# Pinned ScalarE and VectorE queues, a different x load, and a reordered start and end in a DFT + gated MLP kernel

## The chip, the cores and the metric

The kernel runs on one core of one Trainium2 chip. The metric is the device time of one launch in microseconds (us). Five engines have their own instruction queues: PE (TensorE, matmuls; "PEld" is its weight load), DVE (VectorE), ACT (ScalarE), POOL (GpSimd) and SP (SyncE). Transfers go through DMA queues that an engine issues to.

## The reference

```python
x : (8, 3008, 256) f32     w_in : (256, 2048)     w_out : (2048, 256)
X   = fft(fft(x, axis=1), axis=2).real      # along the sequence, then along the channels
h   = X.reshape(24064, 256) @ w_in
g   = h * cos(h)
out = g @ w_out                             # (24064, 256) f32
```

## The kernel before

The DFT along the sequence is done with matmuls on folded inputs (sums and differences of x rows that are gathered in normal and reversed order). The DFT along the channels is folded into `w_in`, giving `Wc` and `Ws`. The MLP then runs in 376 steps: 47 tiles of 256 columns with 8 steps each. A batch is 47 steps, and beside these steps the next batch is loaded, folded (16 folds on DVE, 0.95 us each) and transformed (four groups of matmuls).

One step does this, with the names that the profile shows:

- PE: even matmuls (`hp<-Rr,Wc`, and `hp<-Rl,Wl`, which adds one extra channel in bf16 limbs), odd matmuls (`hp<-Ir,Ws`, into the same PSUM tile), and the second layer's matmuls of four steps earlier (`Ma` to `Md`), of which two groups read a tile `d`.
- ACT: `pt` copy (-2·hp, between the even and the odd matmuls), `h` copy (after the odd ones), rounding, sine, `d` copy.
- DVE: "minus" (`h<-pt,hp`), subtraction of the rounded value (`r<-h,r`), product (`h<-h,r`), two sums.
- POOL: it issues an adding DMA `d<-h`, once a step.

The odd matmuls must wait for the `pt` copy, because they write on into the tile that it reads. Three parts matter below. First the load of x:

```python
    def load_x(b):
        L = [spool.tile([128, 6 * ND], FP, tag=f"xl{j}", bufs=1, ...) for j in range(4)]
        for j in (2, 1):                       # rows in reversed order: a table of row numbers
            nc.gpsimd.indirect_dma_start(
                out=L[j], out_offset=None, in_=xflat,
                in_offset=bass.IndirectOffsetOnAxis(ap=ix[:, j - 1 : j], axis=0),
                element_offset=b * SEQ * ND,
            )
        # row 0 of L[1] is not what the table gives: it is written over
        nc.gpsimd.dma_start(out=L[1][0:1, 0 : 5 * ND], in_=xrows(b, SEQ - 5, 1, 1, 5))
        nc.gpsimd.dma_start(out=L[1][0:1, 5 * ND :], in_=xrows(b, 0, 1, 1, 1))
        nc.sync.dma_start(out=L[0], in_=xrows(b, 0, 6, 128))
        nc.sync.dma_start(out=L[3], in_=xrows(b, HALF, 6, 128))
```

Second, the step's work on ACT and DVE. Only the matmuls are pinned to source order; the instructions of ACT and DVE are not, and are scheduled by the compiler:

```python
        # in mlp1_even, after the even matmuls
        nc.scalar.activation(out=pt, in_=hp, func=AF.Copy, bias=0.0, scale=-2.0)
    ...
        # in mlp1_odd, after the odd matmuls
        nc.scalar.copy(out=h[:, 0:512], in_=hp)
        nc.vector.tensor_tensor(out=h[:, 1023:511:-1], in0=pt, in1=hp, op=ALU.add)   # minus
        act_chain(h, 1024)              # ACT round, DVE subtract, ACT sine, DVE product
        nc.vector.tensor_tensor(out=A[5], in0=A[3], in1=A[2], op=ALU.add)            # sums
        nc.vector.tensor_tensor(out=A[4], in0=A[0], in1=A[5], op=ALU.add)
        d = spool.tile([128, 512], FP, tag="d", bufs=DB, name="d")                   # DB = 4
        nc.scalar.copy(out=d, in_=h[:, 0:512])
        nc.gpsimd.dma_start(out=d, in_=h[:, 768:1280], accum_op=ALU.add)
```

Third, the loop and what runs beside it:

```python
    at(2, load_ext)                     # the extra channel, as 4-byte elements
    at(8, fold_ext); at_dft(10, dft_ext)
    for n in range(3): at(12 + n, lambda n=n: limb_ext(n))
    at(14, lambda: spread_ext(0, RUN))  # gives Rl, first needed at step 16
    for b in range(1, NB):
        s0 = (b - 1) * steps_b
        at(s0 + (7 if b == 1 else 1), lambda b=b: start_batch(b))            # load_x
        for i, key in enumerate(FOLDS):
            at(s0 + 10 + i * 3 // 4, lambda key=key: state["ops"][key]())
    ...
    for i in range(total + LAG):        # LAG = 4
        for fn in side.get(i, ()):
            fn()
        ... mlp1_even(step i)
        ... mlp2(step i - LAG, between=odd)   # odd matmuls before its fourth matmul group
```

## Time and profile before

| | before |
|---|---|
| time | 2174.08 us, median of 2 runs (2171.41 to 2176.75) |
| span of the profiled run, mean granted TensorE clock | 2171.1 us, 0.988 |
| PE busy | 95% |
| first even matmul / step 16 (by its Rl matmul) / last matmul | 60.2 / 166.6 / 2162.2 us |
| 47 steps in the middle | about 257 us |
| step when PE alone limits it | 4.97 us |

The page's first lines give the span, then for each engine its busy time, the share of the span and the number of instructions:

```profile
span 2171.1 us, 26759 instructions
PE 2071.5 (95%) x9540; PEld 1688.2 (78%) x9540; DVE 1723.5 (79%) x2419; ACT 1461.0 (67%) x1976; POOL 353.5 (16%) x414
```

The view of waits lists which engine and tile waited, for whom, and then microseconds in total, how often, and the longest. These are PE's rows:

```profile
PE Mb L378 <- issue: 21.7, 1, 21.7
PE hp L653 <- ACT pt L642: 19.6, 63, 0.9
...
PE hp L632 <- DMA Rl<-r_124: 8.5, 1, 8.5
PE db L831 <- DVE h L690: 7.4, 1, 7.4
```

PE is close to full. Its waits are at the start (the first transform, 21.7; the extra channel's `Rl` at step 16, 8.5), at the end (7.4, the middle tokens), and a small one for the `pt` copy.

In some stretches a step is longer than 4.97 us. The timeline of ACT shows start, duration, engine, line, operation and what it waited for in brackets; this is one such stretch:

```profile
2049.90 0.58 ACT L642 ACTIVATE pt<-hp 128x512 f32<-128x512 f32 x1
2051.29 1.15 ACT L687 ACTIVATE r<-r,halfpi 128x1024 f32<-128x1024 f32 x1 [0.81 <-DVE r L684]
2052.34 0.57 ACT L666 COPY h<-hp 128x512 f32<-128x512 f32 x1
2053.73 0.62 ACT L672 COPY d<-h 128x512 f32<-128x512 f32 x1 [0.82 <-DVE h L690]
2054.32 1.06 ACT L681 ACTIVATE r<-h 128x1024 int32<-128x1024 f32 x1
2055.29 0.58 ACT L642 ACTIVATE pt<-hp 128x512 f32<-128x512 f32 x1
```

From one `pt` copy to the next is 5.39 us. The order is pt, sine, h copy, d copy, round. The commonest step of the kernel is PE's own 4.97 us (144 of 375, from one `hp<-Rl` matmul to the next step's); 5.39 us is found 45 times.

### The profile page before, as it was taken

How to read it: one execution, taken by the hardware profiler on the slowest of the kernel's cores; microseconds unless marked ns; L12 is line 12 of the kernel's file. 1: busy time of each engine (PE TensorE's matmuls, PEld its weight loads, DVE VectorE, ACT ScalarE, POOL GpSimd, SP SyncE). 2: the span in 40 equal slices, each digit the busy share in tenths (PEclk: the TensorE clock that was granted, in tenths of full speed). 3: DMA queues.
4: the chain of work that ended last, by engine and by line, in shares of the span. 5: the costliest groups of instructions: out<-in, count | busy, mean ns of one | idle time of the engine just before them, and what ended most of it. 6: DMA issues, size and time to landing. Idle time of an engine off the chain costs nothing.

```text
span 2171.1 us, 26759 instructions
## 1 busy us (share of the span) xinstructions
PE 2071.5 (95%) x9540; PEld 1688.2 (78%) x9540; DVE 1723.5 (79%) x2419; ACT 1461.0 (67%) x1976; POOL 353.5 (16%) x414
## 2 busy tenths in 40 slices
PE   4878999999999999999999999999999999999988
PEld 1667888877888788887888878887788887888866
DVE  3788778887779778898788977799777987788756
ACT  1656667776676667776677766777667776777755
POOL 1111111111111111111111111111111111111111
PEclk8999999999999999999999999999999999999999
DMA  9934333343333433333333434334333332233323
GB/s 227 68 69 88 55 83 68 64 92 64 76 66 59 89 79 66 65 62 84 84 68 64 89 57 93 61 61 93 71 76 59 63 69 54 55 63 69 62 44 64
DMA packets 212822, 159.85 MB, mean 74 GB/s; under 512 B 159171, under 2 KB 159196, under 8 KB 212175
## 3 DMA queue, kind: packets, MB, share of 16 engines
q0 software_dynamic: 56960, 111.22, 27.8%
q1 hardware_dynamic: 153494, 46.83, 10.6%
q8 instruction: 75, 1.23, 0.2%
q10 hardware_dynamic: 2232, 0.07, 0.1%
q14 instruction: 61, 0.49, 0.1%
HBM read 34.71 MB, written 24.78 MB: 27 GB/s over the span
## 4 chain that ended last, share of the span: by engine, by line
PE 44%; DVE 29%; ACT 19%; issue 5%; DMA 2%; DVEq 0%; SPq 0%; ACTq 0%
DVE h L690 10%; DVE r L684 8%; ACT r L687 8%; PE hp L653 8%; ACT r L681 7%; PE hp L620 7%; PE Md L720 7%; PE Mc L720 6%; PE Mb L720 6%; PE Ma L720 3%; PE db L378 3%; PE da L378 3%; ACT d L672 3%; DVE h L667 2%; PE hp L632 2%
## 5 line engine op out<-in xcount | busy, mean ns | idle before, releaser
L690 DVE SCALAR_TENSOR_TENSOR h<-h,r 128x1024 f32<-128x1024 f32 x377 | 454.9, 1217 | 204.7 <-ACT r L687 202.9
L673 POOL DMA_DIRECT2D d<-h x376 | 321.9, 886 | 1711.3 <-ACT r L681 641.1
L687 ACT ACTIVATE r<-r,halfpi 128x1024 f32<-128x1024 f32 x377 | 431.2, 1146 | 180.4 <-DVE r L684 178.0
L684 DVE TENSOR_TENSOR r<-h,r 128x1024 f32<-128x1024 f32 x377 | 454.7, 1218 | 116.9 <-ACT r L681 116.3
L681 ACT ACTIVATE r<-h 128x1024 int32<-128x1024 f32 x377 | 391.7, 1053 | 84.7 <-DVE h L667 83.7
L653 PE MATMUL hp<-Ir,Ws 127*128 127x256 f32 x1504 | 396.1, 389 | 22.4 <-ACT pt L642 19.6
L620 PE MATMUL hp<-Rr,Wc 128*128 128x256 f32 x1504 | 387.1, 380 | 1.7 <-DVE h L667 1.3
L672 ACT COPY d<-h 128x512 f32<-128x512 f32 x376 | 231.8, 617 | 180.9 <-DVE h L690 170.9
L653 PEld LDWEIGHTS hp<-Ir,Ws 127*128 127x128 f32 x1504 | 268.1, 189 | 105.3 <-ACT pt L642 75.6
L620 PEld LDWEIGHTS hp<-Rr,Wc 128*128 128x128 f32 x1504 | 284.7, 190 | 50.1 <-DVE h L667 5.4
L667 DVE TENSOR_TENSOR h<-pt,hp 128x512 f32<-128x512 f32 x376 | 252.4, 681 | 51.1 <-ACT h L666 50.6
L642 ACT ACTIVATE pt<-hp 128x512 f32<-128x512 f32 x376 | 221.1, 588 | 94.1 <-PE hp L632 91.6
L666 ACT COPY h<-hp 128x512 f32<-128x512 f32 x376 | 217.2, 578 | 95.6 <-PE hp L653 89.5
L720 PE MATMUL Mc<-h,T_118 128*128 128x256 f32 x752 | 224.6, 380 | 4.7 <-DVE X L751 4.7
L720 PE MATMUL Mc<-d,T_120 128*128 128x256 f32 x752 | 223.4, 379 | 4.6 <-DVE h L667 3.5
L720 PE MATMUL Mb<-h,w_88 128*128 128x256 f32 x752 | 224.4, 380 | 3.3 <-DVE X L751 3.3
L720 PE MATMUL Md<-h,T_121 128*128 128x256 f32 x752 | 224.6, 380 | 2.9 <-DVE X L751 1.9
L720 PE MATMUL Ma<-h,w_88 128*128 128x256 f32 x752 | 225.1, 381 | 0.0
L720 PE MATMUL Mb<-h,T_119 128*128 128x256 f32 x752 | 224.1, 380 | 0.0
L720 PE MATMUL Md<-d,w_88 128*128 128x256 f32 x752 | 224.1, 380 | 0.0
L720 PEld LDWEIGHTS Mc<-h,T_118 128*128 128x128 f32 x752 | 142.9, 191 | 25.7 <-issue 6.3
L720 PEld LDWEIGHTS Mc<-d,T_120 128*128 128x128 f32 x752 | 141.7, 189 | 25.7 <-DVE h L667 3.9
(347 smaller groups left out, 1917.6 us busy)
## 6 DMA issues: line engine op xcount, KB each, us to landing
d<-h POOLq DMA_DIRECT2D x376, 256.0 KB, 3.3
out_dram<-tr SPq DMA_DIRECT2D x252, 64.0 KB
h<-in_moe_w_in_dram SPq DMA_DIRECT2D x4, 512.0 KB
w_88<-in_moe_w_out_dram SPq DMA_DIRECT2D x8, 256.0 KB
out_dram<-tr SPq DMA_DIRECT2D x128, 4.0 KB
out_dram<-tr SPq DMA_DIRECT2D x32, 56.0 KB
out_dram<-tr SPq DMA_DIRECT2D x32, 48.0 KB
out_dram<-tr SPq DMA_DIRECT2D x32, 40.0 KB
```

The costliest lines, as they stand in the source:

```text
L620: nc.tensor.matmul(hp[:, i * TW : (i + 1) * TW], lhsT=Wc[:, f * 128 : (f + 1) * 128], rhs=Rr[:, pos : pos + TW], start=(i == 0), stop=Fals ...
L642: nc.scalar.activation(out=pt, in_=hp, func=AF.Copy, bias=0.0, scale=-2.0)
L653: nc.tensor.matmul(hp[:, i * TW : (i + 1) * TW], lhsT=Ws[0:127, f * 128 : (f + 1) * 128], rhs=Ir[:, pos : pos + TW], start=False, stop=Tru ...
L666: nc.scalar.copy(out=h[:, 0:512], in_=hp)
L667: nc.vector.tensor_tensor(out=h[:, 1023:511:-1], in0=pt, in1=hp, op=ALU.add)
L672: nc.scalar.copy(out=d, in_=h[:, 0:512])
L673: nc.gpsimd.dma_start(out=d, in_=h[:, 768:1280], accum_op=ALU.add)
L681: nc.scalar.activation(out=k, in_=h[:, 0:n], func=AF.Copy, bias=0.25, scale=1.0)
L684: nc.vector.tensor_tensor(out=r[:, 0:n], in0=h[:, 0:n], in1=k, op=ALU.subtract)
L687: nc.scalar.activation(out=r[:, 0:n], in_=r[:, 0:n], func=AF.Sin, bias=halfpi, scale=TWO_PI)
L690: nc.vector.scalar_tensor_tensor(out=h[:, 0:n], in0=h[:, 0:n], scalar=TWO_PI, in1=r[:, 0:n], op0=ALU.mult, op1=ALU.mult,)
L720: nc.tensor.matmul(T.M[bank][:, half * TW : (half + 1) * TW], lhsT=lhsT[:, s], rhs=rhs, start=(s == 0 and n in (0, 1, 3, 5)), stop=(s == 7 ...
```

## The change

The intent is to start the steps earlier, to end sooner, and to run the queues of ACT and DVE as a fixed software pipeline over three steps, so that no instruction stands in front of one that is needed sooner. The core of the diff:

```diff
-DB = 4
+DB = 3
 ...
-    neg = SEQ - 5 - 6 * p
-    neg[0] = SEQ - 6
+    neg = SEQ - 5 - 6 * (p + 1)
+    neg[127] = 0
 ... load_x: row 0 no longer gathered and written over; 127 rows are gathered
-        for j in (2, 1):
+        for j, p0 in ((2, 0), (1, 1)):
             nc.gpsimd.indirect_dma_start(
-                out=L[j],
+                out=L[j][p0:],
                 out_offset=None,
                 in_=xflat,
-                in_offset=bass.IndirectOffsetOnAxis(ap=ix[:, j - 1 : j], axis=0),
+                in_offset=bass.IndirectOffsetOnAxis(
+                    ap=ix[: 128 - p0, j - 1 : j], axis=0
+                ),
                 element_offset=b * SEQ * ND,
             )
-        nc.gpsimd.dma_start(out=L[1][0:1, 0 : 5 * ND], in_=xrows(b, SEQ - 5, 1, 1, 5))
-        nc.gpsimd.dma_start(out=L[1][0:1, 5 * ND :], in_=xrows(b, 0, 1, 1, 1))
+        nc.sync.dma_start(out=L[1][0:1, 0 : 5 * ND], in_=xrows(b, SEQ - 5, 1, 1, 5))
+        nc.sync.dma_start(out=L[1][0:1, 5 * ND :], in_=xrows(b, 0, 1, 1, 1))
 ... start: w_out loaded after all DFT constants; limb masks first on ACT's queue; the
     weight row goes to memory and back on POOL's queue, its limbs are made
     (row_to_limbs) behind the first folds and at step 1 rather than ahead of the folds
 ... mlp2: the odd matmuls two places later, Md<-h ahead of Mc<-d
-            if n == 3 and between is not None:
+            if n == 5 and between is not None:
 ... end: the middle tokens in five stages, one a step, rather than all at once
-    at(last, middle_tokens)
+    for i, fn in enumerate((middle_1, middle_2, middle_3, middle_4, middle_5)):
+        at(last + i + (i > 2), fn)
 ... folds: one a step (before: four in three steps)
-            at(s0 + 10 + i * 3 // 4, lambda key=key: state["ops"][key]())
+            at(s0 + 10 + i, lambda key=key: state["ops"][key]())
 ... the loop; every instruction below is now pinned to source order on its engine
     for i in range(total + LAG):
+        stage(i - 1, minus)                    # DVE
         for fn in side.get(i, ()):             # folds and evacuations among them
             fn()
+        stage(i - 2, act_sine)                 # ACT        (calls shortened here)
+        stage(i - 1, rounded)                  # ACT
+        stage(i - 2, act_product)              # DVE
+        stage(i - 2, sums)                     # DVE, then ACT's d copy and the DMA d<-h
+        stage(i - 1, act_rest)                 # DVE        subtraction
+        if ahead < i:
+            stage(i, mlp1_even)                # PE
+            stage(i, copy_even)                # ACT        pt copy
 ...     second layer of step i - LAG on PE, with mlp1_odd(i) inside it
+        stage(i, copy_plus)                    # ACT        h copy
```

More of the change, by code (lines that the diff above doesn't have):

```diff
@@ L130 @@
     nc.sync.dma_start(out=ix, in_=IX_dr.ap())
+    LC = cpool.tile([128, 4], FP, tag="LC")
+    nc.scalar.dma_start(out=LC, in_=LC_dr.ap())
     def load_x(b):
@@ L181 @@
             MC[ri, kodd] = m
-        if kodd == 0:
-            w2r = w2.rearrange("p (q e a j) -> p q e a j", e=2, a=4, j=32)
-            wor = moe_w_out.rearrange("(q p) (a e j) -> p q e a j", p=128, e=2, j=32)
-            for e in range(2):
-                for a in range(4):
-                    nc.sync.dma_start(out=w2r[:, :, e, a], in_=wor[:, :, e, a])
-    LC = cpool.tile([128, 4], FP, tag="LC")
-    nc.sync.dma_start(out=LC, in_=LC_dr.ap())
+    w2r = w2.rearrange("p (q e a j) -> p q e a j", e=2, a=4, j=32)
+    wor = moe_w_out.rearrange("(q p) (a e j) -> p q e a j", p=128, e=2, j=32)
+    for e in range(2):
+        for a in range(4):
+            nc.sync.dma_start(out=w2r[:, :, e, a], in_=wor[:, :, e, a])
     halfpi = cpool.tile([128, 1], FP, tag="halfpi")
@@ L205 @@
     Wl = cpool.tile([128, NDFF], BF, tag="Wl")
-    nc.gpsimd.memset(Rl, 0.0)
-    nc.gpsimd.memset(Wl, 0.0)
+    nc.vector.memset(Wl, 0.0)
+    nc.vector.memset(Rl, 0.0)
     T1 = cpool.tile([128, NF // 2, 128], FP, tag="T1")
@@ L252, in fold_weights, with load_row, row_to_limbs @@
             if q % 2:
-                c0 = (q - 1) * 512
-                half_limbs(slice(c0, c0 + 1024), c0 // 128)
+                load_row(q // 2)
         with nc.allow_non_contiguous_dma(reason="one row to columns"):
-            nc.scalar.dma_start(
+            nc.gpsimd.dma_start(
                 out=wex, in_=wx_dr.rearrange("o (f p) -> p (o f)", p=128)
             )
-    def half_limbs(cols, f0):
-        nc.scalar.dma_start(out=wx_dr[:, cols], in_=Ws[127:128, cols])
+    def load_row(half):
+        cols = slice(half * 1024, (half + 1) * 1024)
+        nc.gpsimd.dma_start(out=wx_dr[:, cols], in_=Ws[127:128, cols])
         wf = spool.tile([8, 128], FP, tag="wf", bufs=2, name="wf")
-        nc.scalar.dma_start(
+        nc.gpsimd.dma_start(
             out=wf, in_=wx_dr[0, cols].rearrange("(f p) -> f p", p=128)
         )
+        state["wf", half] = wf
+    def row_to_limbs(half):
+        cols = slice(half * 1024, (half + 1) * 1024)
         l3 = spool.tile([8, 3, 128], BF, tag="l3", bufs=2, name="l3")
-        split_limbs(wf, [l3[:, j] for j in range(3)])
-        for j in range(3):
-            nc.scalar.dma_start(
-                out=wl_dr[j, cols].rearrange("(f p) -> f p", p=128), in_=l3[:, j]
-            )
+        split_limbs(state["wf", half], [l3[:, j] for j in range(3)])
+        nc.gpsimd.dma_start(
+            out=wl_dr[:, cols].rearrange("j (f p) -> f j p", p=128), in_=l3
+        )
         for i in range(3):
-            nc.scalar.dma_start(out=Wl[3 * i : 3 * i + 3, cols], in_=wl_dr[:, cols])
+            nc.gpsimd.dma_start(out=Wl[3 * i : 3 * i + 3, cols], in_=wl_dr[:, cols])
     def split_limbs(x, limbs):
@@ L521, in limb_ext @@
         rx = X1[:, 0:HALF]
-        limb = spool.tile([128, 3072], BF, tag="C", bufs=1, name="lx")[0:NB, 0:HALF]
+        limb = X0.bitcast(BF)[:, (n % 2) * 1536 : (n % 2) * 1536 + HALF]
         pin(nc.vector.tensor_copy(out=limb, in_=rx))
@@ L640, in mlp1_even, with copy_even @@
             )
-        pt = spool.tile([128, 512], FP, tag="pt", bufs=2, name="pt")
-        nc.scalar.activation(out=pt, in_=hp, func=AF.Copy, bias=0.0, scale=-2.0)
         T.hp[s] = hp
-        T.pt[s] = pt
+    def copy_even(T, s):
+        T.pt[s] = spool.tile([128, 512], FP, tag="pt", bufs=2, name="pt")
+        pin(
+            nc.scalar.activation(
+                out=T.pt[s], in_=T.hp[s], func=AF.Copy, bias=0.0, scale=-2.0
+            )
+        )
     def mlp1_odd(T, s):
         pos = (T.q * TW) % RING
-        hp, pt = T.hp.pop(s), T.pt.pop(s)
         for i in range(2):
@@ L653, in mlp1_odd @@
                 nc.tensor.matmul(
-                    hp[:, i * TW : (i + 1) * TW],
+                    T.hp[s][:, i * TW : (i + 1) * TW],
                     lhsT=Ws[0:127, f * 128 : (f + 1) * 128],
@@ L661, in mlp1_odd, with copy_plus @@
             )
-        h = spool.tile([128, 1536], FP, tag="h", bufs=HB, name="h")
-        A = [h[:, i * TW : (i + 1) * TW] for i in range(6)]
-        nc.scalar.copy(out=h[:, 0:512], in_=hp)
-        nc.vector.tensor_tensor(out=h[:, 1023:511:-1], in0=pt, in1=hp, op=ALU.add)
-        act_chain(h, 1024)
-        nc.vector.tensor_tensor(out=A[5], in0=A[3], in1=A[2], op=ALU.add)
-        nc.vector.tensor_tensor(out=A[4], in0=A[0], in1=A[5], op=ALU.add)
+    def copy_plus(T, s):
+        T.h[s] = spool.tile([128, 1536], FP, tag="h", bufs=HB, name="h")
+        pin(nc.scalar.copy(out=T.h[s][:, 0:512], in_=T.hp[s]))
@@ new lines, in minus, with rounded, sums @@
+    def minus(T, s):
+        pin(
+            nc.vector.tensor_tensor(
+                out=T.h[s][:, 1023:511:-1],
+                in0=T.pt.pop(s),
+                in1=T.hp.pop(s),
+                op=ALU.add,
+            )
+        )
+    def rounded(T, s):
+        r = spool.tile([128, 1024], FP, tag="r", bufs=2, name="r")
+        T.r[s] = r
+        act_round(T.h[s], r, 1024)
+    def sums(T, s):
+        A = [T.h[s][:, i * TW : (i + 1) * TW] for i in range(6)]
+        pin(nc.vector.tensor_tensor(out=A[5], in0=A[3], in1=A[2], op=ALU.add))
+        pin(nc.vector.tensor_tensor(out=A[4], in0=A[0], in1=A[5], op=ALU.add))
@@ L671, in mlp1_odd, with act_round @@
         d = spool.tile([128, 512], FP, tag="d", bufs=DB, name="d")
-        nc.scalar.copy(out=d, in_=h[:, 0:512])
-        nc.gpsimd.dma_start(out=d, in_=h[:, 768:1280], accum_op=ALU.add)
-        T.g[s] = A
+        pin(nc.scalar.copy(out=d, in_=T.h[s][:, 0:512]))
+        pin(nc.gpsimd.dma_start(out=d, in_=T.h[s][:, 768:1280], accum_op=ALU.add))
         T.d[s] = d
-    def act_chain(h, n):
-        r = spool.tile([128, 1024], FP, tag="r", bufs=2, name="r")
+    def act_round(h, r, n):
+        pin(
+            nc.scalar.activation(
+                out=r[:, 0:n].bitcast(I32), in_=h[:, 0:n], func=AF.Copy, bias=0.25, scale=1.0
+            )
+        )
@@ L680, in act_chain, with act_rest @@
+    def act_rest(h, r, n):
         k = r[:, 0:n].bitcast(I32)
-        nc.scalar.activation(
-            out=k, in_=h[:, 0:n], func=AF.Copy, bias=0.25, scale=1.0
-        )
-        nc.vector.tensor_tensor(
-            out=r[:, 0:n], in0=h[:, 0:n], in1=k, op=ALU.subtract
-        )
-        nc.scalar.activation(
-            out=r[:, 0:n], in_=r[:, 0:n], func=AF.Sin, bias=halfpi, scale=TWO_PI
-        )
-        nc.vector.scalar_tensor_tensor(
-            out=h[:, 0:n],
-            in0=h[:, 0:n],
-            scalar=TWO_PI,
-            in1=r[:, 0:n],
-            op0=ALU.mult,
-            op1=ALU.mult,
+        pin(
+            nc.vector.tensor_tensor(
+                out=r[:, 0:n], in0=h[:, 0:n], in1=k, op=ALU.subtract
+            )
+        )
@@ L697, in act_chain, with act_sine, act_product @@
+    def act_sine(r, n):
+        pin(
+            nc.scalar.activation(
+                out=r[:, 0:n], in_=r[:, 0:n], func=AF.Sin, bias=halfpi, scale=TWO_PI
+            )
+        )
+    def act_product(h, r, n):
+        pin(
+            nc.vector.scalar_tensor_tensor(
+                out=h[:, 0:n],
+                in0=h[:, 0:n],
+                scalar=TWO_PI,
+                in1=r[:, 0:n],
+                op0=ALU.mult,
+                op1=ALU.mult,
+            )
         )
@@ L705, in mlp2 @@
             }
-        A, d = T.g.pop(s), T.d.pop(s)
+        h, d = T.h.pop(s), T.d.pop(s)
+        A = [h[:, i * TW : (i + 1) * TW] for i in range(6)]
         parts = (
@@ L711, in mlp2 @@
             ("Mc", 0, T1, A[5]),
+            ("Md", 1, T4, A[2]),
             ("Mc", 1, T3, d[:, 0:256]),
-            ("Md", 1, T4, A[2]),
             ("Md", 0, B22, d[:, 256:512]),
@@ L723, in mlp2 @@
                     rhs=rhs,
-                    start=(s == 0 and n in (0, 1, 3, 5)),
+                    start=(s == 0 and n in (0, 1, 3, 4)),
                     stop=(s == 7),
@@ L728, in mlp2 @@
             )
-        if s == 7:
-            combine(T)
     def combine(T):
         X = spool.tile([128, 1536], FP, tag="C", bufs=1, name="X")
-        nc.scalar.copy(out=X[:, 1280:1536], in_=T.M["Ma"][:, 0:TW])
+        pin(nc.scalar.copy(out=X[:, 1280:1536], in_=T.M["Ma"][:, 0:TW]))
         def blocks(t):
@@ L750, in combine, with turn @@
         ):
-            nc.vector.tensor_tensor(out=o, in0=a, in1=b, op=ALU.add)
+            pin(nc.vector.tensor_tensor(out=o, in0=a, in1=b, op=ALU.add))
         T.X = X
-    def turn(T):
-        C = T.X
-        for sg in range(2):
-            tr = spool.tile([128, 512], FP, tag="ob", bufs=2, name="tr")
+    def turn(T, sg):
+        tr = spool.tile([128, 512], FP, tag="ob", bufs=2, name="tr")
+        pin(
             nc.vector.transpose(
                 out=tr.rearrange("p (b e j) -> p e b j", e=2, j=32),
-                in_=C[:, sg * 512 : (sg + 1) * 512].rearrange(
+                in_=T.X[:, sg * 512 : (sg + 1) * 512].rearrange(
                     "p (e b j) -> p e b j", e=2, j=32
@@ L764, in turn @@
             )
-            store(T, sg, tr)
+        )
+        store(T, sg, tr)
     def store(T, sg, tr):
@@ L804, in store, with middle_1 @@
             j += n
-    def middle_tokens():
+    NM = NF * NB
+    def middle_1():
         pm = dps("da")
         for f in range(NF):
-            nc.tensor.matmul(
-                pm[:, f * NB : (f + 1) * NB],
-                lhsT=Wc[:, f * 128 : (f + 1) * 128],
-                rhs=R4,
-                start=True,
-                stop=True,
-            )
-        n = NF * NB
-        h = spool.tile([128, 6 * ND], FP, tag="xl0", bufs=1, name="h")
-        e = spool.tile([128, 6 * ND], FP, tag="xl1", bufs=1, name="em")[:, 0:n]
-        ev = e.rearrange("p (f b) -> p f b", b=NB)
-        nc.vector.tensor_tensor(
-            out=ev,
-            in0=Rb4.unsqueeze(1).to_broadcast([128, NF, NB]),
-            in1=wex.unsqueeze(2).to_broadcast([128, NF, NB]),
-            op=ALU.mult,
-        )
-        nc.vector.tensor_tensor(out=h[:, 0:n], in0=e, in1=pm[:, 0:n], op=ALU.add)
-        act_chain(h, n)
+            pin(
+                nc.tensor.matmul(
+                    pm[:, f * NB : (f + 1) * NB],
+                    lhsT=Wc[:, f * 128 : (f + 1) * 128],
+                    rhs=R4,
+                    start=True,
+                    stop=True,
+                )
+            )
+        h, e, r = (
+            spool.tile([128, 6 * ND], FP, tag=f"xl{j}", bufs=1, name="hm")[:, 0:NM]
+            for j in range(3)
+        )
+        state["mid"] = pm, h, e, r
@@ new lines, in middle_2 @@
+    def middle_2():
+        pm, h, e, r = state["mid"]
+        ev = e.rearrange("p (f b) -> p f b", b=NB)
+        pin(
+            nc.vector.tensor_tensor(
+                out=ev,
+                in0=Rb4.unsqueeze(1).to_broadcast([128, NF, NB]),
+                in1=wex.unsqueeze(2).to_broadcast([128, NF, NB]),
+                op=ALU.mult,
+            )
+        )
+        pin(nc.vector.tensor_tensor(out=h, in0=e, in1=pm[:, 0:NM], op=ALU.add))
+        act_round(h, r, NM)
+        act_rest(h, r, NM)
@@ L829, in middle_tokens, with middle_3, middle_4 @@
+    def middle_3():
+        _, h, e, r = state["mid"]
+        act_sine(r, NM)
+        act_product(h, r, NM)
+    def middle_4():
+        h = state["mid"][1]
         po = dps("db")
         for f in range(NF):
-            nc.tensor.matmul(
-                po[0:NB, 0:ND],
-                lhsT=h[:, f * NB : (f + 1) * NB],
-                rhs=w2[:, f * ND : (f + 1) * ND],
-                start=(f == 0),
-                stop=(f == NF - 1),
-            )
-        ob = spool.tile([128, 512], FP, tag="ob", bufs=2, name="ob")
@@ L839, in middle_tokens, with middle_5 @@
-        nc.scalar.copy(out=ob[0:NB, 0:ND], in_=po[0:NB, 0:ND])
+            pin(
+                nc.tensor.matmul(
+                    po[0:NB, 0:ND],
+                    lhsT=h[:, f * NB : (f + 1) * NB],
+                    rhs=w2[:, f * ND : (f + 1) * ND],
+                    start=(f == 0),
+                    stop=(f == NF - 1),
+                )
+            )
+        state["po"] = po
+    def middle_5():
+        ob = spool.tile([128, 512], FP, tag="bs", bufs=2, name="mo")
+        pin(nc.scalar.copy(out=ob[0:NB, 0:ND], in_=state["po"][0:NB, 0:ND]))
@@ L859 @@
         ops[key]()
+    row_to_limbs(0)
     done_x = dft_first(xb, banks=("Ma", "Mb"))
@@ L889, in start_batch @@
         state["EO"], state["ops"] = fold_x(load_x(b))
+    at(1, lambda: row_to_limbs(1))
     for n in range(4):
-        at(n, lambda n=n: sum_weights(n))
+        at((1, 2, 3, 3)[n], lambda n=n: sum_weights(n))
     at_dft(2, lambda: dft_R(0, 1, EO))
@@ L911 @@
     total = n_tiles * 8
-    last = total - 12
+    last = total - 14
     def spread4():
@@ L925, in tile_of, with stage @@
         q, s = divmod(i, 8)
-        if s == 0 and q not in tiles:
+        if q not in tiles:
             T = Tile()
             T.q = q
-            T.g, T.d, T.hp, T.pt = {}, {}, {}, {}
+            T.h, T.d, T.hp, T.pt, T.r = {}, {}, {}, {}, {}
             tiles[q] = T
         return tiles[q], s
-    even_done = odd_done = 0
+    def stage(i, fn):
+        if 0 <= i < total:
+            fn(*tile_of(i))
+    ahead = -1
     for i in range(total + LAG):
+        stage(i - 1, minus)
         for fn in side.get(i, ()):
             fn()
-        ends = i >= LAG and (i - LAG) % 8 == 7
-        if even_done <= i < total:
-            mlp1_even(*tile_of(i))
-            even_done = i + 1
-        def odd():
-            nonlocal odd_done
-            while odd_done < even_done:
-                mlp1_odd(*tile_of(odd_done))
-                odd_done += 1
-        if i >= LAG:
-            T, s = tile_of(i - LAG)
-            mlp2(T, s, None if ends else odd)
-            if s == 7:
-                del tiles[T.q]
-                done = T
-        if ends and even_done < total:
-            mlp1_even(*tile_of(even_done))
-            even_done += 1
-        odd()
-        if i >= LAG and (i - LAG) % 8 == 0 and i > LAG:
-            turn(done)
-    turn(done)
+        stage(i - 2, lambda T, s: act_sine(T.r[s], 1024))
+        stage(i - 1, rounded)
+        stage(i - 2, lambda T, s: act_product(T.h[s], T.r.pop(s), 1024))
+        stage(i - 2, sums)
+        stage(i - 1, lambda T, s: act_rest(T.h[s], T.r[s], 1024))
+        if ahead < i:
+            stage(i, mlp1_even)
+            stage(i, copy_even)
+        j = i - LAG
+        ends = j % 8 == 7
+        if j >= 0:
+            T, s = tile_of(j)
+            mlp2(T, s, None if ends else lambda: stage(i, mlp1_odd))
+            if ends:
+                del tiles[T.q]
+                stage(i + 1, mlp1_even)
+                combine(T)
+                stage(i + 1, copy_even)
+                ahead = i + 1
+                stage(i, mlp1_odd)
+                for sg in range(2):
+                    at(i + 2 + sg, lambda T=T, sg=sg: turn(T, sg))
+        else:
+            stage(i, mlp1_odd)
+        stage(i, copy_plus)
+    for sg in range(2):
+        turn(T, sg)
 _INS = ['x', 'moe_w_in', 'moe_w_out']
```

## The prediction

> **What bounds it.** The page shows PE 95%, DVE 79%, ACT 67% busy. Adding up matmul start-to-start times at full speed (215 ns for 256 f32 columns) gives 2021 us of PE work in a 2171 us span: about 135 us of PE waiting, 15 us at the ends. By time (timeline): 57 us before t=200, some 60 us over 200–2000, 15 us in 2000–2100 (middle tokens). A step costs PE 4.97 us; 47 steps with four transforms should cost 249 us and take about 257. In the waits view PE's largest steady wait is the odd matmuls (hp<-Ir,Ws) for ACT's copy pt: 19.6 us (75.6 us on the weight load).
>
> **Start-up.** PE idles from 25 to 46.6 us, because DVE's queue has the weight limbs (waiting 25.7 + 9.4 us for row DMAs) ahead of the folds. With them behind, the transform starts near 25 us and the first step near 37 instead of 60. Much is given back: the extra channel's load is 24,576 packets of 4 bytes, moving from 45 to 105 us in the DMA records; it cannot end before about 100. The Trainium skill ("DMA: Bandwidth & Descriptors", Specifications) wants 512 B for line rate; this trace agrees: 2 GB/s in 45–65 us at 97% DMA share. fold_ext at step 8 now waits for it in a fixed DVE queue. The 8.5 us wait for Rl at step 16 goes. Net gain by t≈170: 20 us (10–30).
>
> **End.** Staged middle tokens remove 7.4 + 1.7 us before their second matmuls, 3 us before the first: 10–13 us.
>
> **Steady state: here I expect a loss.** The queues become strictly ordered (the skill, "TensorE: Matmul & The Clock Gate", Architectural detail: ScalarE and VectorE are strict FIFO; no run yet tests it). ACT's order per step is now sine(i-2), round(i-1), d copy(i-2), pt copy(i), h copy(i). That closes a loop through PE: h copy(i-1) 0.50 → sine 1.18 → DVE product 1.26 → d copy to pt copy 0.52 → pt copy to PE 0.65 → odd matmuls until ACT can start 1.16. All are start-to-start times from the trace: 5.27 us, above PE's 4.97. (The same reading of the old order gives 5.38 for its slow loop; the trace shows steps of 5.39.) Moving the odd matmuls two places later does not help: the loop does not depend on where they stand. A tile's end costs 6.9 us, then two steps 9.9 by DVE's order. So a tile of eight steps costs 6.9 + 9.9 + 5×5.27 = 43.1 us, against about 41.1 before, 39.8 ideal. Transform steps absorb 0.3 us each; their evacuation costs 0.4. Over some 44 tiles: +80 us or so.
>
> **Sum.** 2174 − 20 − 12 + 80 ≈ 2220 us; range 2155 to 2252. Faster 0.13, same 0.37, slower 0.50.
>
> **What would show it.** First mlp1 matmul near 37 us; a stall around steps 8–10, ending at the extra channel's landing, 100–110; ordinary steps of 5.2–5.3 us with hp<-Ir,Ws waiting 0.3 us for pt in nearly each, the chain passing sine, product, d copy, pt copy; 43 us per tile; no 7.4 us wait near the end.
>
> **What would make it wrong.** Hops 0.05 us shorter bring the loop to PE's pace and the kernel to about 2165. If instructions do not stand in source order on ACT, the loop is not there, and steady state could reach PE's pace: 2090–2120. If the extra channel lands earlier, start-up gains 10 us more.

## More of the kernel before

The load of x in the middle of the kernel looks like this on POOL's timeline and in the DMA view of 528 to 545 us (40 slices of 0.425 us; the last line gives the KB of one transfer and the median time from issue to landing):

```profile
530.69 1.05 POOL L139 DMA_INDIRECT xl_3530<-in_x_dram,ix  x1 [0.79 <-PE da L378]
...
535.87 0.54 POOL L146 DMA_DIRECT2D xl_3530<-in_x_dram  x1 [1.10 <-DMA xl_3530<-in_x_dram,ix]
```

```profile
GB/s 0 0 0 0 0 53 202 198 164 0 116 0 275 434 405 419 241 145 207 198 48 24 10 0 0 0 0 0 0 0 0 0 0 0 0 0 202 202 202 10
d<-h POOLq DMA_DIRECT2D x3, 256.0 KB, 3.6
```

The gather of 128 rows of 6,144 bytes moves at over 400 GB/s and has landed by 535.9, when the transfer that mends row 0 starts. The `d` transfers around it land in 3.6 us.

## The result, and the profile after

| | before | after |
|---|---|---|
| time, median of 2 | 2174.08 us | 2509.62 us (2506.40 to 2512.85) |
| ratio | | 1.154 (95%: 1.146 to 1.163) |
| span, granted clock | 2171.1, 0.988 | 2504.3, 0.947 |
| step 16 | 166.6 | 232.7 |
| 47 steps in the middle | about 257 us | about 298 us |

Ratios are the mean time of one kernel's runs over that of the other's of the same rounds, so they are not quite the ratio of the medians that are quoted.

The kernel became 15% slower, far outside the predicted range. The page and PE's waits:

```profile
span 2504.3 us, 26460 instructions
PE 2146.3 (86%) x9540; PEld 1711.9 (68%) x9540; DVE 1782.5 (71%) x2421; ACT 1435.5 (57%) x1976; POOL 364.6 (15%) x409
```

```profile
PE hp L663 <- ACT pt L652: 153.7, 152, 8.5
PE Mc L760 <- DMA d<-h: 139.7, 7, 35.3
PE Mb L384 <- DVE xb L359: 31.9, 1, 31.9
```

Two kinds of waits have grown. The first was predicted: for the `pt` copy (19.6 us before), in many steps. The second was not: seven waits for the `d` transfer that take 20 us each on average, the longest 35.3, and one of 31.9 us at the start for a fold. In the view of waits of all engines that fold's row names its own cause, the gather of x:

```profile
DVE xa L359 <- DMA xl_77<-in_x_dram,ix: 39.8, 1, 39.8
```

The page's table of DMA issues hides the second kind. Its median for `d<-h` went from 3.3 us to 3.2, because only a few of the 376 transfers are late.

One of the seven waits, on the timelines of POOL and PE, and the DMA view of 645 to 690 us (slices of 1.125 us):

```profile
647.11 2.64 POOL L143 DMA_INDIRECT xl_3506<-in_x_dram,ix  x1 [0.30 <-issue]
...
667.49 0.84 POOL L700 DMA_DIRECT2D d<-h  x1 [6.16 <-DVE h L697]
690.01 0.86 POOL L700 DMA_DIRECT2D d<-h  x1 [21.68 <-ACT d L699]
```

```profile
686.99 1.22 PE L760 MATMUL Mc<-d,T_120 128*128 128x256 f32 x2 [17.15 <-DMA d<-h]
```

```profile
GB/s 0 0 191 47 15 15 23 27 27 27 151 111 27 27 22 217 56 27 22 27 186 366 269 129 27 100 161 34 28 23 28 28 23 28 28 18 13 12 13 7
d<-h POOLq DMA_DIRECT2D x4, 256.0 KB, 25.2
xl_3506<-in_x_dram,ix POOLq DMA_INDIRECT x1, 38.4
```

Under the bursts lies a floor of 22 to 28 GB/s that lasts for over 30 us. It is the gather: 127 rows of 6,144 bytes in the 33 us of its packets are 23.6 GB/s. From the third batch on, the gathers of 128 rows take 2.3 to 5.2 us of packets, those of 127 rows 31 to 34 us (41 and 51 in the first two batches). The `d` transfers issued behind it land after 25.2 us rather than 3.6. The records of single packets show why: each `d` transfer writes 128 packets of 2,048 bytes. For the three transfers issued while the gather ran, at 655.18, 660.47 and 667.49, 120 packets each land on time, and the remaining 8 each, 24 together, only from 685 on. Eight in 128 is one sixteenth. So a sixteenth of each of them stands behind the gather, as if the gather were all on one of sixteen DMA engines. The packets of this gather also come one after the other: in its 34 us two are under way together for only 0.3 us, while in the gather of 128 rows at 530.69 us in the kernel before, 16 at once is the commonest state. The records do not name the engine; that it is one is inferred from the rate, from this share and from the packets' order.

The Trainium skill has the rule that fits. "DMA: Bandwidth & Descriptors", section "Why a DMA increments its semaphore by 16 and not by 1", says that the number of engines is the largest k up to 16 that divides the sizes of the slowest dimension, and gives 128 partitions as k = 16 and "127 partitions or a `[1, 1]` scalar → 1". It adds an exception for some direct copies issued by GpSimd, where 127 partitions do get all engines, and says nothing of indirect gathers. This trace agrees with the rule for the gather. The page's Specifications give about 27 GiB/s (29 GB/s) for an engine; the gather's own rate here is 23.6 GB/s.

The predicted kind of wait is seen on the three timelines of an ordinary step, first ACT, then DVE, then PE:

```profile
1012.66 0.59 ACT L677 COPY h<-hp 128x512 f32<-128x512 f32 x1 [1.22 <-PE hp L663]
1013.14 1.15 ACT L721 ACTIVATE r<-r,halfpi 128x1024 f32<-128x1024 f32 x1
...
1015.63 0.62 ACT L699 COPY d<-h 128x512 f32<-128x512 f32 x1 [0.39 <-issue]
1016.15 0.59 ACT L652 ACTIVATE pt<-hp 128x512 f32<-128x512 f32 x1
1017.96 0.59 ACT L677 COPY h<-hp 128x512 f32<-128x512 f32 x1 [1.22 <-PE hp L663]
```

```profile
1014.33 1.23 DVE L728 SCALAR_TENSOR_TENSOR h<-h,r 128x1024 f32<-128x1024 f32 x1 [0.36 <-ACT r L721]
```

```profile
1016.80 1.13 PE L663 MATMUL hp<-Ir,Ws 127*128 127x256 f32 x4
```

Read from start to start: h copy 1012.66, sine +0.48, product +1.19, d copy +1.30, pt copy +0.52, odd matmuls +0.65, next h copy +1.16. The sum is 5.30 us, and nothing in it leaves the circle. PE needs 4.97.

### The profile page after: what moved, and what is told of

It is laid out like the page before. It is cut to its first block, busy times and chain, and to the rows that moved or that the text cites. A ratio compares the mean times of both kernels' runs of the same rounds, so it can differ in the third digit from the quotient of the medians. Undisturbed runs are those within 1.5% of the kernel's fastest.

```text
span 2504.3 us, 26460 instructions
## 1 busy us (share of the span) xinstructions
PE 2146.3 (86%) x9540; PEld 1711.9 (68%) x9540; DVE 1782.5 (71%) x2421; ACT 1435.5 (57%) x1976; POOL 364.6 (15%) x409
## 5 line engine op out<-in xcount | busy, mean ns | idle before, releaser
L681 DVE TENSOR_TENSOR h<-pt,hp 128x512 f32<-128x512 f32 x376 | 258.4, 687 | 516.5 <-ACT h L677 516.5
L663 PE MATMUL hp<-Ir,Ws 127*128 127x256 f32 x1504 | 422.9, 404 | 160.2 <-ACT pt L652 153.7
L626 PE MATMUL hp<-Rr,Wc 128*128 128x256 f32 x1504 | 397.6, 388 | 1.1 <-DVE Rr L399 1.1
L760 PE MATMUL Mc<-d,T_120 128*128 128x256 f32 x752 | 234.6, 394 | 139.7 <-DMA d<-h 139.7
L626 PEld LDWEIGHTS hp<-Rr,Wc 128*128 128x128 f32 x1504 | 293.5, 195 | 50.9 <-DVE Rr L399 1.7
L760 PEld LDWEIGHTS Mc<-d,T_120 128*128 128x128 f32 x752 | 147.3, 197 | 163.3 <-DMA d<-h 143.0
L760 PE MATMUL Md<-d,w_90 128*128 128x256 f32 x752 | 231.7, 391 | 0.0
L697 DVE TENSOR_TENSOR h<-h 128x256 f32<-128x256 f32 x376 | 159.9, 425 | 12.9
```

What stands on the lines that cost most here:

```text
L626: nc.tensor.matmul(hp[:, i * TW : (i + 1) * TW], lhsT=Wc[:, f * 128 : (f + 1) * 128], rhs=Rr[:, pos : pos + TW], start=(i == 0), stop=Fals ...
L663: nc.tensor.matmul(T.hp[s][:, i * TW : (i + 1) * TW], lhsT=Ws[0:127, f * 128 : (f + 1) * 128], rhs=Ir[:, pos : pos + TW], start=False, sto ...
L681: nc.vector.tensor_tensor(out=T.h[s][:, 1023:511:-1], in0=T.pt.pop(s), in1=T.hp.pop(s), op=ALU.add,)
L760: nc.tensor.matmul(T.M[bank][:, half * TW : (half + 1) * TW], lhsT=lhsT[:, s], rhs=rhs, start=(s == 0 and n in (0, 1, 3, 4)), stop=(s == 7 ...
```

## The experiments

Eleven kernels were run. All outputs are right. E5, E6, E7 and E9 ran on another chip than the rest. Times are medians; the time of the kernel before in the same rounds was 2173.06 to 2174.17 us throughout.

| run | what | us | ratio to before (95%) |
|---|---|---|---|
| e1_gather128 | after, old x load | 2328.32 | 1.071 (1.069–1.073) |
| e2_before_gather127 | before, new x load | 2350.01 | 1.080 (1.078–1.083) |
| e3_split112_15 | after, the 127 rows as 112 + 15 | 2335.20 | 1.075 (1.072–1.077) |
| e4_pt_first | E1, pt copy ahead of the d copy | 2143.74 | 0.986 (0.983–0.989) |
| e5_fold_early | E1, folds ahead of minus | 2284.18 | 1.050 (1.048–1.052) |
| e6_pt_first_fold_early | E4 and E5 together | 2143.59 | 0.986 (0.984–0.988) |
| e7_pt_first_ext_late | E4, extra channel's work later | 2139.24 | 0.983 (0.982–0.985) |
| e8_rest_first | E7, subtraction ahead of the sums | 2114.68 | 0.974 (0.972–0.975) |
| e9_before_startup | before, new start alone | 2173.31 | 1.000 (0.999–1.002) |
| e10_rest_first_fold_early | E8 and folds ahead of minus | 2118.74 | 0.975 (0.973–0.976) |
| e11_odd_at_3 | E1, odd matmuls at their old place | 2369.34 | 1.091 (1.089–1.094) |

The theories were these. G: the gather of 127 rows costs the time of the long waits for `d` and of the late start. L: the fixed order on ACT, with the pt copy behind the d copy, which waits for the product, is a loop of 5.3 us. The rivals: that the three `d` buffers (DB = 3) cause the waits for `d`; that the new place of the odd matmuls causes the `pt` waits; that the new queues at the start make the loss. (The expectations call G "Theory A", and the fixed queues with three `d` buffers "Theory R".)

### E1: the old x load in the new kernel

```diff
-        for j, p0 in ((2, 0), (1, 1)):
+        for j in (2, 1):
             nc.gpsimd.indirect_dma_start(
-                out=L[j][p0:],
+                out=L[j],
 ... and the old row table and the old mending of row 0
```

> The changed kernel with only the x load put back (second gather over 128 partitions, its first row mended afterwards). Theory A (the 127-partition gather runs on one DMA engine and the accumulating d transfers queue behind it there): the seven waits of the Mc matmuls for d (140 us in the changed kernel) fall under 5 us, the 32 us wait for xb before the first transform falls under 8 us, and the time falls by 160 to 220 us, to 2290-2350 us. Theory R (the fixed queues alone are at fault, the d waits being their consequence with three d buffers instead of four): the time stays within 30 us of 2510. My predicted 2220 would need steps without folds to be all of the loss; I expect more, as fold steps are 5.7 us.

It measured 2328.32 us, so the gather is worth 181.3 us of the change. PE's longest waits are now:

```profile
PE hp L659 <- ACT pt L648: 166.6, 157, 11.7
...
PE Mc L756 <- DMA d<-h: 1.2, 1, 1.2
```

The waits for `d` fell from 139.7 to 1.2 us, with DB = 3 unchanged. So the three buffers are not at fault. The wait for `pt` stayed. Even without the gather the kernel is far above the predicted range, which ends at 2252 us.

### E2: the new x load in the kernel before

```diff
-        for j in (2, 1):
+        for j, p0 in ((2, 0), (1, 1)):
             nc.gpsimd.indirect_dma_start(
-                out=L[j],
+                out=L[j][p0:],
 ... and the new row table, and the mending of row 0 on SP's queue
```

> The kernel before with only the new x load (second gather over 127 partitions). Theory A: 100 to 150 us slower than before, 2270-2330 us, with the matmuls that read d waiting some 15 us once per batch, and the 127 packets of 6 KB spread over some 35 us instead of 3 us. Theory R: within 25 us of 2174.

It measured 2350.01 us, 176.6 above the kernel before of the same rounds. Alone in the old kernel, the load costs about what it costs in the new one, more than the 100 to 150 us that I had expected, and the same wait appears:

```profile
PE Mc L724 <- DMA d<-h: 149.6, 8, 41.9
```

### E3: 127 rows, but gathered as 112 and 15

This tells whether it is the missing row, the queue of the mending transfers, or the number 127. Everything of the changed kernel is kept, and only the gather is cut in two, of 112 rows (a multiple of 16) and of 15:

```diff
-        for j, p0 in ((2, 0), (1, 1)):
+        for j, p0, n, c in ((2, 0, 128, 1), (1, 1, 112, 0), (1, 113, 15, 2)):
             nc.gpsimd.indirect_dma_start(
-                out=L[j][p0:],
+                out=L[j][p0 : p0 + n],
 ...
-                    ap=ix[: 128 - p0, j - 1 : j], axis=0
+                    ap=ix[:n, c : c + 1], axis=0
```

> The changed kernel with its 127-row gather cut into two gathers of 112 and 15 partitions, same rows, same places, nothing else. If the number of partitions of one gather sets how many engines it uses: the time is within 30 us of e1_gather128 and the d waits are gone. If something else of the new load is at fault (the row indices, the mending rows on another queue, 127 rows as such): it stays within 30 us of 2510.

It measured 2335.20 us; its interval overlaps that of E1, and PE's waits for `d` are 1.6 us in total:

```profile
PE Mc L761 <- DMA d<-h: 1.6, 1, 1.6
```

The packets of the 127 rows now take 3.0 to 5.2 us from the third batch on, and 15 or 16 of them at once is the commonest state. The same 127 rows, in two pieces, cost nothing to speak of, with the first piece still starting at partition 1 and the mending still on SP's queue. It is the number 127 in one gather, as the skill's rule has it (112 would give 16 engines and 15 would give 15).

### E4: the pt copy ahead of the d copy, in E1

Theory L says that the loop exists only because ACT's `pt` copy stands behind the `d` copy, which waits for DVE's product. The order on PE and DVE stays as it was; on ACT it becomes sine, round, pt, d, h.

```diff
         stage(i - 1, rounded)
+        if ahead < i:
+            stage(i, mlp1_even)
+            stage(i, copy_even)
         stage(i - 2, act_product)        # calls shortened
         stage(i - 2, sums)
         stage(i - 1, act_rest)
-        if ahead < i:
-            stage(i, mlp1_even)
-            stage(i, copy_even)
```

> e1_gather128 with ScalarE's order per step sine, round, pt copy, d copy, h copy (pt copy moved ahead of the d copy, nothing else). If the loop h copy - sine - product - d copy - pt copy - odd matmuls sets the step: ordinary steps fall from 5.31 to 4.97 us, fold steps from 5.72 to about 5.0, the waits of the odd matmuls for pt fall from about 150 us to under 40, a tile costs about 41 us, and the time is 100 to 160 us under e1_gather128. If DVE's load or the order at a tile's end sets the pace instead: within 30 us of e1_gather128.

It measured 2143.74 us, 184.6 less than E1, and 1.4% less than the kernel before. ACT's timeline now closes at PE's pace:

```profile
1001.13 0.59 ACT L673 COPY h<-hp 128x512 f32<-128x512 f32 x1 [1.92 <-PE hp L659]
...
1003.99 0.59 ACT L648 ACTIVATE pt<-hp 128x512 f32<-128x512 f32 x1
1004.65 0.62 ACT L695 COPY d<-h 128x512 f32<-128x512 f32 x1
1006.10 0.59 ACT L673 COPY h<-hp 128x512 f32<-128x512 f32 x1 [0.84 <-PE hp L659]
```

From h copy to h copy is 4.97 us, even with an evacuation between. So one adjacent order on one engine was worth 185 us. That ACT and DVE execute in strict order, which the skill states in "TensorE: Matmul & The Clock Gate", section "Architectural detail: the array is 16× 32×32, not 1× 128×128", is what the argument rests on. This run agrees with it for ACT; the runs that change only DVE's order are E5 and E8.

The loop that I had worked out saves 0.33 us a step, 125 us in 376 steps. The other 60 us needed a reason, which the next run looks for. PE's largest wait left was 15.4 us once, at step 9, when DVE waited for the extra channel:

```profile
PE hp L659 <- ACT pt L648: 57.5, 46, 15.4
```

```profile
108.33 0.93 DVE L566 TENSOR_TENSOR XA<-Rr,Ir 8x752 f32<-8x752 f32 x1 [13.59 <-DMA Ir<-in_x_dram]
```

### E5: the folds ahead of minus, in E1

In E1, as in the changed kernel, a step with a fold takes 5.72 us rather than 5.30. Here are two h copies of E1's ACT timeline and DVE's work in the step between:

```profile
968.12 0.58 ACT L673 COPY h<-hp 128x512 f32<-128x512 f32 x1 [1.22 <-PE hp L659]
...
973.84 0.58 ACT L673 COPY h<-hp 128x512 f32<-128x512 f32 x1 [1.22 <-PE hp L659]
```

```profile
968.74 0.69 DVE L677 TENSOR_TENSOR h<-pt,hp 128x512 f32<-128x512 f32 x1 [0.98 <-ACT h L673]
969.35 0.95 DVE L317 SCALAR_TENSOR_TENSOR xl<-xl 128x762 f32<-128x762 f32 x1
970.21 1.22 DVE L724 SCALAR_TENSOR_TENSOR h<-h,r 128x1024 f32<-128x1024 f32 x1
```

DVE was idle for 0.98 us, then did minus, then the fold, and the product started 1.60 us after the sine (968.61) rather than 1.19. DVE had enough free time for the fold, but at another place of the queue: ahead of minus, where it waits for ACT's h copy to end. Minus and the h copy both read the PSUM tile `hp`, and in all 376 steps of the kernel before, the one after, E1 and E4, minus starts at least 31 ns after the end of the h copy. The two readers never overlap. The skill's "PSUM — Partial Sum Buffer", section "PSUM bank collisions raise a hardware error", says that two engines must be kept apart on one bank and quadrant, reads against reads included; the traces agree that they are kept apart. Both instructions also write the tile `h`, in different halves; no run separates the two possible reasons for the wait.

The edit puts the fold into that free time:

```diff
     for i in range(total + LAG):
+        for fn in early.get(i, ()):      # the folds, and nothing else
+            fn()
         stage(i - 1, minus)
         for fn in side.get(i, ()):
             fn()
```

> e1_gather128 with each x fold put ahead of minus in VectorE's queue (it then runs in the time that VectorE idles for the h copy) instead of between minus and the product. My missed term would be this: minus starts only after the h copy has ended (0.62 us, not together with it), so a fold after it pushes the product back by 0.42 us, 5.72 instead of 5.31 a step. Expected: fold steps 5.31, tiles with folds near 43.4 us instead of 47-50, time 45 to 85 us under e1_gather128, 2240-2285 us, which is what my prediction had for the loop alone. If VectorE's load as such makes fold steps long: within 20 us of e1_gather128.

It measured 2284.18 us, 44.1 less than E1, just under the 45 to 85 that I had expected. DVE's timeline shows the fold in the free time, and the product again 1.19 us behind the sine (1004.45):

```profile
1003.53 0.95 DVE L312 TENSOR_TENSOR xl<-xl,xl 128x768 f32<-128x768 f32 x1
1004.59 0.69 DVE L677 TENSOR_TENSOR h<-pt,hp 128x512 f32<-128x512 f32 x1
1005.64 1.23 DVE L724 SCALAR_TENSOR_TENSOR h<-h,r 128x1024 f32<-128x1024 f32 x1 [0.36 <-ACT r L717]
```

Steps with folds fell to 5.31 us. 112 folds at 0.41 us are 46 us, which fits the 44. Of the 60 us some 16 are left open. The step after a tile's end, which falls from 6.77 us in E1 to 5.75 in E4 in plain tiles, by more than the loop's 0.33, may hold them; that was not summed.

### E6: E4 and E5 together

The edits are those of E4 and E5.

> e4_pt_first with each x fold ahead of minus. With the loop already broken a fold costs only at tile ends (6.53, 5.25, 5.25 us against 5.76, 4.97, 4.97), 1.3 us in some 16 tiles: 10 to 25 us under e4_pt_first, 2120-2135 us. If VectorE is full in those steps whatever the order: within 6 us of e4_pt_first.

It measured 2143.59 us, the same as E4. The gain that I expected did not come. Once the product is not on the circle, the fold's place in ordinary steps is off the critical path, and the steps at a tile's end stayed at 6.54, 5.25 and 5.25 us. The 44 us of E5 exist only inside the loop.

### E7: the extra channel's work later, in E4

```diff
-    at(8, fold_ext)
-    at_dft(10, dft_ext)
+    at(11, fold_ext)
+    at_dft(13, dft_ext)
     for n in range(3):
-        at(12 + n, lambda n=n: limb_ext(n))
-    at(14, lambda: spread_ext(0, RUN))
+        at((14, 14, 15)[n], lambda n=n: limb_ext(n))
+    at(15, lambda: spread_ext(0, RUN))
```

> e4_pt_first with the extra channel's fold moved from step 8 to 11, its transform from 10 to 13, its limbs from 12-14 to 14-15. If the 15.4 us wait at step 9 comes from the fixed VectorE queue standing at that fold until the 4-byte load lands (108 us), the wait falls to under 5 us, new waits (for xe or Rl) stay under 6 us, and the time is 6 to 15 us under e4_pt_first. If the whole chain from the load's landing to Rl sets the time, the wait only moves: within 4 us.

It measured 2139.24 us, 4.5 less than E4, where I had expected 6 to 15. The longest wait for `pt` fell from 15.4 to 5.9 us, but new ones of 4.3 us (even matmuls for minus) and 2.3 us (`Ma` for a tile's result) came in the view of waits.

The intervals of the ratios of E4 and E7 overlap (0.983–0.989 and 0.982–0.985), so the gain is likely and small.

### E8: the subtraction ahead of the sums, in E7

Of DVE's five instructions in a step, the two sums are needed late (by the second layer two steps on), and the subtraction is what the next sine waits for.

```diff
         stage(i - 2, act_product)        # calls shortened
-        stage(i - 2, sums)
         stage(i - 1, act_rest)
+        stage(i - 2, sums)
```

> e7_pt_first_ext_late with VectorE's subtraction (rest of i-1) ahead of the two sums of i-2, nothing else. At a tile's end the chain h copy - sine - product - sums - rest - sine - round - pt copy - odd matmuls is 8.9 us by my sum of durations against 8.0 of PE work; taking the sums (0.8 us) out of it should bring the 5.76 us step after a tile's end to 4.97, a plain tile from 40.6 to 39.8 us, and the time down by 20 to 38 us, to 2101-2120. If the tile's end is set by the combine's four additions instead: within 8 us of e7.

It measured 2114.68 us, ratio 0.974, 24.6 us less than E7. This is the best version, and it beats both kernels. PE is busy for 97% of its span of 2111.6 us.

```profile
PE hp L659 <- ACT pt L648: 21.6, 23, 5.3
```

The wait for `pt` was halved. The step after a tile's end, where four additions of the tile's results come on DVE on top, went from 5.75 to 5.19 us (with a fold beside it, from 6.54 to 5.85).

### E9: the new start alone, in the kernel before

```diff
+    LC = cpool.tile([128, 4], FP, tag="LC")          # first on ACT's queue
+    nc.scalar.dma_start(out=LC, in_=LC_dr.ap())
 ... w_out after the DFT constants; memsets of Wl and Rl on DVE; load_row and
     row_to_limbs on POOL's queue
     for key in "e1 E0 EO0".split():
         ops[key]()
+    row_to_limbs(0)
     done_x = dft_first(xb, banks=("Ma", "Mb"))
 ...
+    at(1, lambda: row_to_limbs(1))
```

> The kernel before with only the change's start: limbs behind the folds and on the GpSimd queue, w_out loaded last, masks loaded first, memsets on VectorE, weight sums one step later. My prediction gave the start 20 us (10-30) with the landing of the extra channel taking back the rest. Given e4_pt_first, which stands at step 16 only 1 us ahead of before, I now expect 0 to 10 us: 2164-2174 us, first step near 40 us instead of 60, step 16 near 157-167 us.

It measured 2173.31 us against 2174.17, no difference. Step 16 came at 166.5 us, as in the kernel before (166.6). What was gained early was spent in two waits:

```profile
PE hp L634 <- DMA Wl<-wl: 19.2, 1, 19.2
PE hp L634 <- DMA Rl<-r: 8.5, 1, 8.5
```

The weight limbs now go over POOL's queue, where in this kernel POOL first waits 7.6 us for the gather, to mend its row 0, before it can issue the load of `Wl` (71.3 us). And the extra channel still sets when step 16 can go.

### E10: the folds ahead of minus, in E8

The edit is that of E5.

> e8_rest_first with each x fold ahead of minus as in e6. In e6 it gave nothing, since tile-end steps with folds (6.54, 5.25, 5.25) were the same; if those were set by the chain that e8 shortens, e10 stays within 6 us of e8. If VectorE's order matters there once the sums are out of the way: 6 to 15 us under e8.

It measured 2118.74 us, 4 more than E8 with overlapping intervals. The fold's place again does nothing outside the loop; the step after a tile's end is 6.38 us with a fold, against 5.85 in E8.

### E11: the odd matmuls at their old place, in E1

The prediction said that "the loop does not depend on where they stand".

```diff
-            if n == 5 and between is not None:
+            if n == 3 and between is not None:
                 between()
```

> e1_gather128 with the odd matmuls put back to the third place of the second layer's seven (two places earlier, as the kernel before had them). My prediction said that the loop does not depend on where they stand: ordinary steps stay 5.30-5.31, the time within 12 us of e1_gather128. If the place matters, the odd matmuls wait 0.86 us more a step and the time rises by 100 us or more.

Ordinary steps are still 5.30 us, so that statement holds. The kernel measured 2369.34 us, though, 41 more than E1, and I had expected it within 12. PE's wait for `pt` grew from 166.6 us to:

```profile
PE hp L659 <- ACT pt L648: 194.1, 145, 14.3
```

The step after a tile's end became 7.64 us instead of 6.77 in plain tiles. Summed over all tiles this step costs 54 us more and the next one 8 us less, which is nearly all of the 46.5 us between the two profiled runs. So the later place, which I had called of no help, is a gain of the change at the ends of tiles. Whether it is one without the loop was not tested.

## Why the prediction was wrong

**The account.** From the medians, the gather costs 181.3 (after to E1), ACT's order 184.6 (E1 to E4), and what is left of the change gains 29.6 (E4 against before): 336 us, and the measured difference is 335.5. The three terms follow one path from run to run, so their sum says nothing of itself; that the gather's term hardly depends on the path is shown by E2 (176.6 in the old kernel). The 29.6 were not split further: the five stages at the end, the folds' new spacing and `Md<-h` ahead of `Mc<-d` were never run alone.

**The step that failed first: the sum has no term for the load of x.** The prediction says "2174 − 20 − 12 + 80 ≈ 2220". It costs what moved between engines and queues, and passes over the edit from 128 to 127 gathered rows, which looks like a saving: one row less, and two small transfers moved off POOL's queue. It cost +181 us. E2 shows the same (176.6) in the old kernel, and E3 shows that it is the count in one gather. PE's waits for `d` (139.7) and the late start (31.9) are 171.6 us of it. The mean granted clock is lower too (0.947; 0.951 in E2, 0.984 in E1), so it goes with the stalls; how many of the remaining microseconds are slower matmuls after a stall was not separated. The sign of the wrong step was to be had from the skill page that the prediction cites for another purpose.

**The steady state: the mechanism was right, the size was not.** The prediction gave ordinary steps of 5.2 to 5.3 us and the loop of 5.27; they are 5.30, with the same links. It gave 43.1 us a tile; a plain tile takes 43.39. It named the order on ACT, and E4 shows that undoing that order takes the loop away. The term "+80 us or so" was too small. From step 16 to the end, "+80 − 12" means +68; E1, without the gather, measures about +158 by the medians (+148 in the profiled run, E1's fastest). Two things were missing in it:

- The folds. Their steps were taken to cost nothing beyond the loop. They cost 0.41 us each, because minus is held behind the h copy and the free time of DVE lies ahead of it; E5 measures 44 us.
- The difference per tile. Over 313 steps of the middle, E5 is about 104 us above the kernel before. Cut at the `hp<-Rl` matmuls, 57 of them lie in 146 steps with neither fold nor transform (3.1 us for eight of them), 40 in 111 steps with folds (2.9 us for eight) and 7 in the 56 steps of transforms; where a step is cut shifts some microseconds between the three. The prediction had 2.0 for a tile (43.1 − 41.1). By the same count, eight plain steps take 41.0 us before and 44.1 in E5, so it was mainly the new kernel's tile that came out too short. Why those in E5 are longer than a purely plain tile (43.4) was not followed further.

**The start: wrong, and small.** "Net gain by t≈170: 20 us" was not there. In E4, step 16 comes at 165.4 us against 166.6, in E1 at 163.1, in E3, which keeps the change's own queues, at 166.3: a gain of 0 to 4. The parts of the mechanism were right: the first step at 39.4 us in E4 (predicted 37), and DVE held by the extra channel until 108.33 (predicted 100 to 110), as the trace of the 4-byte elements had let one expect. (The 2 GB/s at 97% DMA share that the prediction gives for 45 to 65 us hold from 50 on; 45 to 50 has 16 GB/s at 89%.) What was mis-sized is how much is given back: 15.4 us for `pt` behind that wait, 7.2 us for `Wl`. In the changed kernel itself the gather moved step 16 to 232.7.

**The end: right in kind.** 10 to 13 us were predicted. In E4 the stretch from step 335 to the end is 241.5 us against 250.3, so 8.8 less; the wait of 7.4 us for the middle tokens is gone. The end was not run alone, so a part of this can be E4's other steps.

**Which warnings were of use.** The prediction's "what would make it wrong" lists only ways of being faster. Nothing in it asks which edits had not been costed at all.

## What to carry to other kernels

Cost every edit of a diff, also those that look like a saving: here 127 rows in place of 128 made a gather take 31 to 34 us, and a sixteenth of the `d` transfers behind it was held until it ended, which showed as a wait for an innocent tile. In a queue of fixed order, follow the circle through all engines and put the instruction that another engine waits for ahead of the one that itself waits; here one such exchange was worth 185 us and a second, on DVE, 25. Free time of an engine counts only at the place of the queue where it lies, and using it pays only while that engine is on the circle (44 us in E5, nothing in E6).

## What the Trainium skill lacked or had wrong

- "DMA: Bandwidth & Descriptors" has the rule that 127 partitions go to one engine, and an exception for direct copies from GpSimd, but does not say which holds for an indirect gather from GpSimd. Here the rule holds: 127 rows of 6,144 bytes took 31 to 34 us of packets at some 24 GB/s, 128 rows 2.3 to 5.2 us, and 112 + 15 rows 3.0 to 5.2 us; these cost nothing to speak of (2335.20 us against 2328.32 for the kernel).
- The same page gives no measure of what such a transfer costs the ones behind it. The three `d` transfers issued on the same queue while one gather ran had 8 of their 128 packets each held until it ended: `d<-h` landed after 25.2 us rather than 3.6.
- "PSUM — Partial Sum Buffer" says that two readers of one bank and quadrant are to be kept apart, but not what that costs in a queue. Here the second reader started 31 ns or more after the first one's end in all 376 steps of four kernels, DVE waited 0.98 us for it in ordinary steps of the changed kernel, and work put behind it cost 0.41 us a step (44 us in all), if that rule and not the shared tile `h` is the reason.
- Nothing that these pages state was found wrong; the strict order of ACT and DVE, stated in "TensorE: Matmul & The Clock Gate", agrees with a change of order on ACT alone that moved the time by 184.6 us (E4) and one on DVE alone that moved it by 24.6 (E8).
